# Narrower scatter targets, spread sums and separate last input tiles in a fused attention, expert and feed-forward kernel

## The chip, the cores and the metric

The kernel runs on one core of one Trainium2 chip. The metric is the device time of one execution in microseconds (us); the kernel before has a median of 876.0 us in three runs. Engines are called as the profile calls them: PE (TensorE matmul), DVE (VectorE), ACT (ScalarE), POOL (GpSimd), SP (SyncE, which here only issues DMAs).

## The reference

Three layers follow one another on 2304 tokens (4 sequences of 576) with 512 features: block-causal attention, a layer of 8 experts of which each token takes one, and a dense feed-forward layer with a softplus.

```python
def reference(q, k, v, w_gate, w1, w2, w_in, w_out):
    x = attention(q, k, v)            # 4 x 8 heads, 576 positions, blocks of 64, softmax
    x = x.transpose(0, 2, 1, 3).reshape(2304, 512)
    e = argmax(x @ w_gate, axis=1)    # one expert of 8 for each token
    x = gate_w * (relu(x @ w1[e]) @ w2[e])
    h = x @ w_in                      # 512 -> 2048
    g = maximum(h, 0) + log1p(exp(-abs(h)))
    return g @ w_out                  # 2048 -> 512
```

## The kernel before

All products are made of three matmuls on split operands (high and low part in fp32r): high x high, low x high, high x low. The order of all work is written out by hand in one string of step names, `SCHEDULE`; each name calls one step, and the instructions of a step go to their engines in that order. Pools of named tiles give the buffers; an instruction that writes a tile waits for the last readers of the tile that had the buffer before.

The change lies in the feed-forward layer (`ffn`), the last 410 us. Tokens stand in 18 tiles of 128, which are worked on in five groups: groups 0 to 3 have four tiles each, group 4 has two. In steps called after the group `g`:

- `Pg.f.k` are the matmuls of the first layer for the 16 column blocks `f`, `ag.f.0` to `.2` three activations on ACT (L1242, L1244, L1246), `ag.f.3` the maximum and sum on DVE (L1248), `ag.f.4` the store of the block to a scratch tensor `gd` in DRAM by SP (L1250). The five `ft` tiles go round.
- The second layer is a 2 x 2 scheme with seven products instead of eight. For each of the 8 chunks `c`, `Ng.c.0` loads two blocks of `gd` back into a tile `gq` (two DMAs of SP, L1346), `.1` to `.3` form the sums on DVE (L1352 for the first; L1355 and L1356; L1358), `.4` casts to high parts `ah` on ACT (L1365, L1367) and `.5` forms the low parts `al` on DVE (L1369, L1372). `Qg.c.m` are the seven products on PE. `W` steps load converted weights for it (SP, L1332).
- `og.u.i` combine the products on ACT and DVE (L1405 copies a PSUM bank to a tile `fy`; L1413, L1416, L1418, L1422 write `fos`), `Og.u.j` write the result. For groups 0 to 3 that is a scatter by an indirect DMA of POOL, four in a row for each group (L1430), whose row indices stand in `OI`. For group 4 it is four plain stores of 128 x 256 to rows 2048 to 2303 of `out`, three by SP and one by ACT (L1427).

A tile `gq` takes one of three buffers in turn. Chunks 3 to 5 of group 4 use the second halves of the tiles of chunks 0 to 2, so that chunk 6 gets the buffer that chunks 0 and 3 had, and chunk 7 that of chunks 1 and 4. A scatter names the whole of `out` as its target, so an instruction that writes any part of `out` waits until the scatters before it have landed.

Of the kernel before, what the change touches and what calls it, by code (L numbers as in the profile page):

```python
# [7 lines left out]
F32 = mybir.dt.float32  # L8
# [12 lines left out]
NT, DM, E, F1, F2 = 2304, 512, 8, 1024, 2048  # L21
# [192 lines left out]
a4.6.4 W4.4 W4.5 P4.8.3 a4.7.2 P4.9.0 a4.7.3 a4.8.0 P4.9.1 a4.8.1 a4.7.4 W4.6 W4.7 P4.9.2 a4.8.2 P4.9.3 P4.10.0 a4.8.3  # L214
a4.9.0 P4.10.1 a4.8.4 W4.8 W4.9 a4.9.1 P4.10.2 a4.9.2 P4.10.3 P4.11.0 a4.9.3 a4.10.0 P4.11.1 a4.9.4 W4.10 W4.11 a4.10.1
P4.11.2 a4.10.2 P4.11.3 P4.12.0 a4.10.3 a4.11.0 P4.12.1 a4.10.4 W4.12 W4.13 a4.11.1 P4.12.2 a4.11.2 P4.12.3 P4.13.0
a4.11.3 a4.12.0 P4.13.1 a4.11.4 a4.12.1 P4.13.2 a4.12.2 P4.13.3 P4.14.0 a4.12.3 a4.13.0 P4.14.1 a4.12.4 W5.0 W5.1
a4.13.1 P4.14.2 a4.13.2 P4.14.3 P4.15.0 a4.13.3 N0.2.1 N0.2.2 N0.2.3 a4.14.0 P4.15.1 a4.13.4 W5.2 W5.3 a4.14.1 P4.15.2
a4.14.2 P4.15.3 Q0.0.0 a4.14.3 a4.15.0 a4.14.4 W5.4 W5.5 a4.15.1 Q0.0.1 a4.15.2 a4.15.3 Q0.0.2 a4.15.4 W5.6 e2 N0.1.4
N0.1.5 N0.2.4 N0.4.0 W5.7 W5.8 W5.9 N0.3.1 N0.3.2 N0.3.3 N0.2.5 N0.5.0 W5.10 W5.11 W5.12 W5.13 W6.0 Q0.0.3 Q0.0.4  # L220
Q0.0.5 Q0.0.6 Q0.1.0 N0.3.4 Q0.1.1 N0.4.1 N0.4.2 N0.4.3 Q0.1.2 N0.3.5 N0.6.0 W6.1 W6.2 W6.3 Q0.1.3 Q0.1.4 Q0.1.5 Q0.1.6
# [23 lines left out]
N3.6.5 N4.1.0 N4.3.0 N4.4.0 Q3.4.3 Q3.4.4 Q3.4.5 Q3.4.6 Q3.5.0 N3.7.4 Q3.5.1 N4.0.1 N4.0.2 N4.0.3 Q3.5.2 N3.7.5 N4.2.0  # L245
N4.5.0 Q3.5.3 Q3.5.4 Q3.5.5 Q3.5.6 Q3.6.0 N4.0.4 Q3.6.1 N4.1.1 N4.1.2 N4.1.3 Q3.6.2 N4.0.5 Q3.6.3 Q3.6.4 Q3.6.5 Q3.6.6
Q3.7.0 N4.1.4 N4.2.1 N4.2.2 N4.2.3 N4.1.5 Q3.7.1 o3.0.0 o3.1.0 Q3.7.2 Q3.7.3 o3.0.1 o3.0.2 o3.1.1 o3.1.2 Q3.7.4 Q3.7.5
o3.0.3 o3.1.3 Q3.7.6 o3.0.4 O3.0.0 O3.0.1 o3.1.4 O3.1.0 O3.1.1 Q4.0.0 N4.2.4 Q4.0.1 N4.3.1 N4.3.2 N4.3.3 Q4.0.2 N4.2.5
Q4.0.3 Q4.0.4 Q4.0.5 Q4.0.6 Q4.1.0 N4.3.4 Q4.1.1 N4.4.1 N4.4.2 N4.4.3 Q4.1.2 N4.3.5 N4.6.0 Q4.1.3 Q4.1.4 Q4.1.5 Q4.1.6
Q4.2.0 N4.4.4 Q4.2.1 N4.5.1 N4.5.2 N4.5.3 Q4.2.2 N4.4.5 N4.7.0 Q4.2.3 Q4.2.4 Q4.2.5 Q4.2.6 Q4.3.0 N4.5.4 Q4.3.1 N4.6.1  # L250
N4.6.2 N4.6.3 Q4.3.2 N4.5.5 Q4.3.3 Q4.3.4 Q4.3.5 Q4.3.6 Q4.4.0 N4.6.4 Q4.4.1 N4.7.1 N4.7.2 N4.7.3 Q4.4.2 N4.6.5 Q4.4.3
Q4.4.4 Q4.4.5 Q4.4.6 Q4.5.0 N4.7.4 Q4.5.1 N4.7.5 Q4.5.2 Q4.5.3 Q4.6.0 Q4.6.1 Q4.6.2 Q4.6.3 Q4.7.0 Q4.7.1 o4.0.0 Q4.7.2
Q4.7.3 o4.0.1 O4.0.1 O4.0.2 o4.0.2 Q4.5.4 Q4.5.5 Q4.6.4 Q4.6.5 Q4.7.4 Q4.7.5 o4.0.3 Q4.5.6 Q4.6.6 Q4.7.6 o4.0.4 O4.0.0
# [932 lines left out]
def ffn(tc, P, yd, gd, wd, w_in, w_out, HB, OI, out, ident):  # L1186
# [7 lines left out]
    st = {}  # L1194
# [76 lines left out]
    QW = 256  # L1271
# [63 lines left out]
    def chunk(g, c, i):  # L1335
        w = 128 * groups[g][1]
        q = w // 2
        n = 8 * g + c
        if i == 0:
            p, tag = (P["pa"], f"gq{n % 3}") if n % 3 < 2 else (P["hlb"], "U2")  # L1340
            if g == 4 and 3 <= c < 6:
                t = st["g", g, c] = st["g", g, c - 3][:, :, w:2 * w]
            else:
                t = st["g", g, c] = p.tile([128, 2, 512], F32, tag=tag, name=f"gq{n % 3}", bufs=1)
            for j in range(2):
                nc.sync.dma_start(t[:, j, 0:w], gd[16 * g + c + 8 * j, :, 0:w])  # L1346
            return
        t = st["g", g, c]
        quarter = lambda h, a: t[:, h, q * a:q * a + q]
        if i == 1:  # L1350
            s = st["gs", g, c] = sums(n)
            TT(s[:, 0:w], t[:, 0, 0:w], t[:, 1, 0:w], op=ALU.add)  # L1352
        elif i == 2:
            s = st["gs", g, c]
            TT(s[:, w:w + q], quarter(0, 1), quarter(0, 0), op=ALU.subtract)  # L1355
            TT(s[:, w + q:2 * w], quarter(1, 0), quarter(1, 1), op=ALU.subtract)  # L1356
        elif i == 3:
            TT(st["gs", g, c][:, 2 * w:2 * w + q], quarter(0, 0), quarter(1, 1), op=ALU.add)  # L1358
        else:
            if i == 4:  # L1360
                st["gp", g, c] = part_tiles(n % 3)
            s = st["gs", g, c][:, 0:5 * q]
            h, l = st["gp", g, c]
            if i == 4:
                nc.scalar.copy(h[:, 0:5 * q], s)  # L1365
                for j in range(2):
                    nc.scalar.copy(h[:, (5 + j) * q:(6 + j) * q], quarter(j, j))  # L1367
            else:
                TT(l[:, 0:5 * q], s, h[:, 0:5 * q].bitcast(F32), op=ALU.subtract)  # L1369
                for j in range(2):  # L1370
                    e = slice((5 + j) * q, (6 + j) * q)
                    TT(l[:, e], quarter(j, j), h[:, e].bitcast(F32), op=ALU.subtract)  # L1372
# [51 lines left out]
    def done(g, u, j):  # L1424
        if g == 4:
            i, o = groups[g][0] + j // 2, QW * (j % 2)
            (nc.scalar if j == 3 else nc.sync).dma_start(out[128 * i:128 * i + 128, o:o + QW], st["out", g, u][:, j])  # L1427
            return
        i = groups[g][0] + groups[g][1] // 2 * j + u
        nc.gpsimd.indirect_dma_start(  # L1430
            out=out, out_offset=bass.IndirectOffsetOnAxis(ap=OI[:, i:i + 1], axis=0),
            in_=st["out", g, u][:, 2 * j:2 * j + 2].rearrange("p a b -> p (a b)"), in_offset=None,
            bounds_check=NT - 1, oob_is_err=False,
        )

    calls = {}
# [185 lines left out]
```

## Time and profile before

| | us |
|---|---|
| median of three runs | 876.0 (875.87 to 878.16) |
| the profiled execution: its time | 877.16 |
| the profiled execution: its span | 875.5 |
| PE busy | 861.2 (98%) |
| DVE busy | 667.5 (76%) |
| ACT busy | 559.6 (64%) |
| POOL busy | 124.2 (14%) |

The span runs from the first to the last instruction of the core; 1.7 us of the profiled execution's time lie outside of it. PE's clock was granted in full from beginning to end (each of the 40 slices of the profile shows a 9). A row of the timeline has the start and the duration in us, the engine, the line, the operation, what it writes and reads, and in brackets the idle time of that engine before it with what ended it. An engine name with a q (SPq, POOLq) is its sequencer: waits, DMA issues and the closing instructions of the program stand there.

### The profile page before, as it was taken

The numbers are of one execution on the slowest core, as the hardware profiler recorded it, in microseconds if no ns is written. First come the engines' busy times: TensorE is split into PE (matmuls) and PEld (weight loads), VectorE is DVE, ScalarE is ACT, GpSimd is POOL, SyncE is SP. The second block draws the span as 40 slices with busy tenths as digits, with TensorE's granted clock in tenths as the row PEclk, the third lists the DMA queues.
The fourth block names the chain that finished last, engine by engine and source line by source line (L and its number), as shares of the span: only waits on it lengthen the run. The fifth ranks groups of instructions, "written<-read, shape, count | busy, mean of one in ns | idle before, by whom it ended". The sixth has DMA issues, their size and how long they took to land.

```text
span 875.5 us, 17767 instructions
## 1 busy us (share of the span) xinstructions
PE 861.2 (98%) x5974; PEld 754.4 (86%) x5974; DVE 667.5 (76%) x1627; ACT 559.6 (64%) x1236; POOL 124.2 (14%) x149
## 2 busy tenths in 40 slices
PE   8999999999999999999999999999999999999997
PEld 5778777877899899998998888878889999999997
DVE  5787789977999888665963768667775589897966
ACT  6677777786665767655854878878888643343432
POOL 3010000011032142211311000000000003150302
PEclk9999999999999999999999999999999999999999
DMA  6976196124427398765461566457755884533422
GB/s 135 175 155 139 43 177 187 50 87 143 163 76 228 111 310 277 267 222 193 120 229 39 179 225 215 147 181 251 263 213 210 266 290 128 162 118 127 142 74 97
DMA packets 141941, 149.15 MB, mean 170 GB/s; under 512 B 73487, under 2 KB 99087, under 8 KB 141840
## 3 DMA queue, kind: packets, MB, share of 16 engines
q1 hardware_dynamic: 135696, 132.80, 50.1%
q0 software_dynamic: 4800, 14.70, 4.8%
q8 instruction: 49, 0.80, 0.4%
q10 hardware_dynamic: 1344, 0.43, 0.2%
q14 instruction: 52, 0.43, 0.2%
HBM read 120.09 MB, written 41.43 MB: 184 GB/s over the span
## 4 chain that ended last, share of the span: by engine, by line
PE 65%; DMA 1%; ACT 0%; SPq 0%; issue 0%; DVE 0%; DVEq 0%; ACTq 0%
PE yps L1090 4%; PE yps L1092 4%; PE yps L1091 3%; PE fh L1233 3%; PE fh L1234 3%; PE fh L1232 3%; PE hps L1056 3%; PE hps L1057 3%; PE hps L1055 3%; PE fz L1399 3%; PE fz L1397 3%; PE fz L1398 3%; PE fX L1233 2%; PE fX L1234 2%; PE fX L1232 2%; PE fY L1233 2%
## 5 line engine op out<-in xcount | busy, mean ns | idle before, releaser
L1365 ACT CAST ah<-sum 128x1280 fp32r<-128x1280 f32 (+1 forms) x40 | 46.3, 1158 | 103.1 <-issue 39.4
L410 ACT ACTIVATE P<-s,negm 128x192 f32<-128x192 f32 (+4 forms) x160 | 83.6, 526 | 39.1 <-DVE negm L402 33.8
L1055 PE MATMUL hps<-xh,H1h 128*128 128x256 f32 x320 | 90.7, 283 | 0.0
L1057 PE MATMUL hps<-xh,H1l 128*128 128x256 f32 x320 | 90.5, 283 | 0.0
L1056 PE MATMUL hps<-xl,H1h 128*128 128x256 f32 x320 | 90.5, 283 | 0.0
L402 DVE CUSTOM_DVE_ANT_0 s<-s,mask 128x576 f32<-128x576 f32 (+3 forms) x128 | 70.1, 569 | 26.4 <-PE s L392 23.5
L1011 DVE TENSOR_TENSOR H2l<-R,H2h 128x512 fp32r<-128x512 f32 x96 | 63.7, 686 | 24.9 <-ACT H2h L1007 21.3
L1007 ACT CAST H2h<-R 128x512 fp32r<-128x512 f32 x96 | 57.5, 623 | 28.8 <-PE yps L1091 14.1
L1090 PE MATMUL yps<-H2h,hh 128*128 128x512 f32 x176 | 71.5, 406 | 0.4 <-PEq L1562 0.4
L1430 POOL DMA_INDIRECT out_dram<-fos,OI x16 | 41.0, 2561 | 204.8 <-DVE fos L1422 166.5
L1091 PE MATMUL yps<-H2h,hl 128*128 128x512 f32 x176 | 68.8, 391 | 0.0
L1092 PE MATMUL yps<-H2l,hh 128*128 128x512 f32 x176 | 68.7, 391 | 0.0
L1011 DVE TENSOR_TENSOR H1l<-R,H1h 128x512 fp32r<-128x512 f32 x96 | 62.4, 684 | 8.3 <-ACT H1h L1007 6.3
L1369 DVE TENSOR_TENSOR al<-sum,ah 128x1280 fp32r<-128x1280 f32 (+1 forms) x40 | 54.1, 1352 | 16.9 <-ACT ah L1365 16.9
L1007 ACT CAST H1h<-R 128x512 fp32r<-128x512 f32 x96 | 55.5, 622 | 16.4 <-PE hps L1056 10.3
L420 PE MATMUL pt<-ident,P 128*128 128x128 f32 x400 | 61.1, 281 | 2.1 <-DVE PT L426 0.8
L1056 PEld LDWEIGHTS hps<-xl,H1h 128*128 128x128 f32 x320 | 61.4, 192 | 0.3
L1055 PEld LDWEIGHTS hps<-xh,H1h 128*128 128x128 f32 x320 | 61.3, 192 | 0.3
L1057 PEld LDWEIGHTS hps<-xh,H1l 128*128 128x128 f32 x320 | 61.4, 192 | 0.0
L392 PEld LDWEIGHTS s<-kZ,qZ 64*128 64x128 f32 x576 | 47.3, 185 | 14.0 <-ACT P L410 5.5
L392 PE MATMUL s<-kZ,qZ 64*128 64x288 f32 (+4 forms) x576 | 56.1, 312 | 1.0 <-DVE kZ L367 0.6
L420 PEld LDWEIGHTS pt<-ident,P 128*128 128x128 f32 x400 | 44.3, 141 | 11.1 <-DVE PT L426 4.4
(366 smaller groups left out, 2606.6 us busy)
## 6 DMA issues: line engine op xcount, KB each, us to landing
R<-in_moe_w_dram SPq DMA_DIRECT2D x96, 512.0 KB
gd<-ft SPq DMA_DIRECT2D x64, 256.0 KB
gq<-gd SPq DMA_DIRECT2D x64, 256.0 KB
dbw<-in_moe_w_out_dram SPq DMA_DIRECT2D x32, 256.0 KB
dbl<-in_moe_w_in_dram SPq DMA_DIRECT2D x22, 256.0 KB
yg<-yd SPq DMA_DIRECT2D x4, 1026.0 KB
xd<-xs SPq DMA_DIRECT2D x16, 256.0 KB
wd<-ah SPq DMA_DIRECT2D x4, 896.0 KB
```

Source lines behind the costliest of these rows:

```text
L392: mm(o, lhsT=a, rhs=b, start=first, stop=last)
L402: nc.vector.tensor_tensor_reduce(x, x, MASK[:, S - NK[c]:S], scale=1.0, scalar=3.0e38, op0=ALU.add, op1=ALU.min, accum_out=m)
L410: nc.scalar.activation(t, x, AF.Exp, bias=NM.pop((p, j, c))[0:n], scale=-1.0, accum_out=rs[p % 4][0:n, c, j:j + 1])
L420: nc.tensor.transpose(ps[:, 128 * i:128 * i + 128], PB[p % NPB][c][:, a:a + 128], ident)
L1007: nc.scalar.copy(HW[l, i][0], raw(l, i))
L1011: TT(l_, raw(l, i), h.bitcast(F32), op=ALU.subtract)
L1055: mm(a, lhsT=wh, rhs=xh, start=(k == 0), stop=False)
L1056: mm(a, lhsT=wh, rhs=xl, start=False, stop=False)
L1057: mm(a, lhsT=wl, rhs=xh, start=False, stop=(k == 3))
L1090: mm(o, lhsT=h[:, c], rhs=wh, start=(f == 0), stop=False)
L1091: mm(o, lhsT=l[:, c], rhs=wh, start=False, stop=False)
L1092: mm(o, lhsT=h[:, c], rhs=wl, start=False, stop=(f == 7))
```

## The change

It has three parts. The scatters name only rows 0 to 2047 of `out` as target, and their bound on an index is 2047. In group 0, the four sums of chunk 2 (`N0.2.1` to `N0.2.3`), which stood in a row behind `a4.13.3`, stand one step each behind `a4.11.3`, `a4.12.3` and `a4.13.3`. And the inputs of chunks 6 and 7 of group 4 get tiles of 128 x 2 x 256 under the tag of the two `fy` buffers, with their loads `N4.6.0` and `N4.7.0` at the start of the products of group 4, behind the scatters of group 3.

```diff
-a4.11.3 a4.12.0 P4.13.1 a4.11.4 a4.12.1 P4.13.2 a4.12.2 P4.13.3 P4.14.0 a4.12.3 a4.13.0 P4.14.1 a4.12.4 W5.0 W5.1
-a4.13.1 P4.14.2 a4.13.2 P4.14.3 P4.15.0 a4.13.3 N0.2.1 N0.2.2 N0.2.3 a4.14.0 P4.15.1 a4.13.4 W5.2 W5.3 a4.14.1 P4.15.2
+a4.11.3 N0.2.1 a4.12.0 P4.13.1 a4.11.4 a4.12.1 P4.13.2 a4.12.2 P4.13.3 P4.14.0 a4.12.3 N0.2.2 a4.13.0 P4.14.1 a4.12.4
+W5.0 W5.1 a4.13.1 P4.14.2 a4.13.2 P4.14.3 P4.15.0 a4.13.3 N0.2.3 a4.14.0 P4.15.1 a4.13.4 W5.2 W5.3 a4.14.1 P4.15.2
...
-o3.0.3 o3.1.3 Q3.7.6 o3.0.4 O3.0.0 O3.0.1 o3.1.4 O3.1.0 O3.1.1 Q4.0.0 N4.2.4 Q4.0.1 N4.3.1 N4.3.2 N4.3.3 Q4.0.2 N4.2.5
+o3.0.3 o3.1.3 Q3.7.6 o3.0.4 O3.0.0 O3.0.1 o3.1.4 O3.1.0 O3.1.1 N4.6.0 N4.7.0 Q4.0.0 N4.2.4 Q4.0.1 N4.3.1 N4.3.2 N4.3.3
...
             if g == 4 and 3 <= c < 6:
                 t = st["g", g, c] = st["g", g, c - 3][:, :, w:2 * w]
+            elif g == 4 and c > 5:
+                t = st["g", g, c] = P["p2"].tile([128, 2, QW], F32, tag="fy", name="gq3", bufs=2)
...
         nc.gpsimd.indirect_dma_start(
-            out=out, out_offset=bass.IndirectOffsetOnAxis(ap=OI[:, i:i + 1], axis=0),
+            out=out[0:NT - 256], out_offset=bass.IndirectOffsetOnAxis(ap=OI[:, i:i + 1], axis=0),
             in_=st["out", g, u][:, 2 * j:2 * j + 2].rearrange("p a b -> p (a b)"), in_offset=None,
-            bounds_check=NT - 1, oob_is_err=False,
+            bounds_check=NT - 257, oob_is_err=False,
```

On DVE, at the end of the first layer of group 4 (L1248 is the sum `a4.f.3`; the four lines that read `gq` are the sums of chunk 2 of group 0), the rows stand before the change as

```order
L1248 SCALAR_TENSOR_TENSOR ft<-fh,ft 128x256
L1248 SCALAR_TENSOR_TENSOR ft<-fY_12744,ft 128x256
L1248 SCALAR_TENSOR_TENSOR ft<-fX_12765,ft 128x256
L1352 TENSOR_TENSOR sum_12811<-gq_12657 128x512
L1355 TENSOR_TENSOR sum_12811<-gq_12657 128x256
L1356 TENSOR_TENSOR sum_12811<-gq_12657 128x256
L1358 TENSOR_TENSOR sum_12811<-gq_12657 128x256
```

and with it, two lines further down in the source, as

```order
L1248 SCALAR_TENSOR_TENSOR ft<-fh,ft 128x256
L1354 TENSOR_TENSOR sum_12770<-gq_12657 128x512
L1248 SCALAR_TENSOR_TENSOR ft<-fY_12744,ft 128x256
L1357 TENSOR_TENSOR sum_12770<-gq_12657 128x256
L1358 TENSOR_TENSOR sum_12770<-gq_12657 128x256
L1248 SCALAR_TENSOR_TENSOR ft<-fX_12765,ft 128x256
L1360 TENSOR_TENSOR sum_12770<-gq_12657 128x256
```

The first sum has moved in front of the last but one `ft` row shown, the next two in front of the last, and one stays behind it; nothing else on DVE has moved.

On SP, the last DMAs of the program (two loads each for chunks 6 and 7 of group 4, then the three stores; DMASW are the semaphores of POOL's DMAs, DMAHW those of SP's and ACT's) stand before the change as

```order
L1346 DMA gq_14956<-gd 128x256 [waits DMAHW6_49,DMAHW5_49,DVE_49]
L1346 DMA gq_14956<-gd 128x256
L1346 DMA gq_14993<-gd 128x256 [waits DMAHW7_49,DMAHW0_49,DVE_49]
L1346 DMA gq_14993<-gd 128x256
L1427 DMA out_dram<-fos 128x256 [waits DMASW4_49,DMASW5_49,DMASW3_49,DMASW6_49,DMASW2_49,DMASW7_49,DMASW1_49,DMAHW1_49,DMASW0_49,DVE_49]
L1427 DMA out_dram<-fos 128x256 [waits DMAHW2_49]
L1427 DMA out_dram<-fos 128x256 [waits DMAHW3_49,DVE_49]
```

and with it as

```order
L1348 DMA gq_14896<-gd 128x256 [waits DMAHW5_49,DVE_49,Activation_49]
L1348 DMA gq_14896<-gd 128x256 [waits DMAHW6_49]
L1348 DMA gq_14899<-gd 128x256 [waits DMAHW7_49,DVE_49,Activation_49]
L1348 DMA gq_14899<-gd 128x256 [waits DMAHW0_49]
L1429 DMA out_dram<-fos 128x256 [waits DMAHW1_49,DVE_49]
L1429 DMA out_dram<-fos 128x256 [waits DMAHW2_49]
L1429 DMA out_dram<-fos 128x256 [waits DMAHW3_49,DVE_49]
```

The order on SP is the same; the loads wait for the `fy` tiles of group 3 in place of the older `gq` tiles, and the stores no longer wait for any scatter. ACT's one store loses the same waits. The scatters of POOL keep theirs: each still waits for the one before it.

## Rows read from the trace of the kernel before

**Rows 1.** Windows: each engine's busy us, instruction count, PE clock, DMA share, GB/s.
```profile
690.00:692.00 2.00, 1.08 (x9) 1.08 (x10) 0.84 (x2) 2.00 (x4) 0.00 (x0) 1.00 0.88 262
692.00:870.00 178.00, 178.00 (x1490) 178.00 (x1489) 151.59 (x317) 69.88 (x124) 40.98 (x16) 1.00 0.46 149
```

**Rows 2.** Timeline around PE's one gap, 685 to 691 us: PE, ACT, SP, DVE.
```profile
690.92 0.39 PE L1397 MATMUL fX<-Wh,ah 128*128 128x256 f32 x1 [1.00 <-DVE ft L1248]
...
689.12 0.38 ACT L1242 ACTIVATE ft<-fX 128x256 f32<-128x256 f32 x1 [0.72 <-DMA gd<-ft]
...
686.02 0.38 SPq L1250 DMA_DIRECT2D gd<-ft  x1
...
685.95 0.42 DVE L1248 SCALAR_TENSOR_TENSOR ft<-fY,ft 128x256 f32<-128x256 f32 x1 [0.74 <-ACT ft L1246]
687.12 0.43 DVE L1248 SCALAR_TENSOR_TENSOR ft<-fX,ft 128x256 f32<-128x256 f32 x1 [0.75 <-ACT ft L1246]
687.46 0.68 DVE L1352 TENSOR_TENSOR sum<-gq 128x512 f32<-128x512 f32 x1
```

**Rows 3.** The last stores: SP's wait (total, times, longest), issues, DVE's last work.
```profile
SPq L1427 <- DMA out_dram<-fos,OI: 11.1, 1, 11.1
...
870.32 0.75 DVE L1422 TENSOR_TENSOR fos<-fw,fz 128x256 f32<-128x256 f32 x2 [0.38 <-PE fz L1399]
871.37 1.31 SPq L1427 DMA_DIRECT2D out_dram<-fos  x3
871.41 0.38 ACTq L1427 DMA_DIRECT2D out_dram<-fos  x1
```

**Rows 4.** The program's closing instructions: ns shortest/median/longest, first and last start.
```profile
L1617 POOLq EVENT_SEMAPHORE  x4: 17/17/17, 874.7 to 875.4; - x4
L1617 POOLq DRAIN  x3: 40/113/5882, 868.5 to 875.2; - x3
L1617 SPq DRAIN  x3: 7/7/13, 874.6 to 874.9; - x3
```

**Rows 5.** Timeline of POOL: the second scatter of group 0, the four of group 3.
```profile
736.82 9.11 POOL L1430 DMA_INDIRECT out_dram<-fos,OI  x1 [2.53 <-DMA out_dram<-fos,OI]
...
852.68 0.98 POOL L1430 DMA_INDIRECT out_dram<-fos,OI  x1 [21.15 <-DVE fos L1422]
856.21 3.80 POOL L1430 DMA_INDIRECT out_dram<-fos,OI  x1 [2.54 <-DVE sum L1358]
863.44 1.31 POOL L1430 DMA_INDIRECT out_dram<-fos,OI  x1 [3.43 <-DVE sum L1358]
868.39 0.98 POOL L1430 DMA_INDIRECT out_dram<-fos,OI  x1 [3.63 <-DVE fos L1413]
```

**Rows 6.** Timeline of DVE beside the second scatters of groups 0 and 3.
```profile
745.40 0.69 DVE L1352 TENSOR_TENSOR sum<-gq 128x512 f32<-128x512 f32 x1 [0.33 <-DMA gq<-gd]
...
858.67 0.48 DVE L1372 TENSOR_TENSOR al<-gq,ah 128x128 fp32r<-128x128 f32 x2
859.87 0.43 DVE L1352 TENSOR_TENSOR sum<-gq 128x256 f32<-128x256 f32 x1 [0.72 <-DMA gq<-gd]
...
864.22 0.82 DVE L1369 TENSOR_TENSOR al<-sum,ah 128x640 fp32r<-128x640 f32 x1
864.96 0.48 DVE L1372 TENSOR_TENSOR al<-gq,ah 128x128 fp32r<-128x128 f32 x2
```

**Rows 7.** Windows inside the second scatters of groups 0 and 3, as in rows 1.
```profile
737.40:745.00 7.60, 7.60 (x65) 7.60 (x65) 7.60 (x15) 2.71 (x7) 7.60 (x1) 1.00 0.44 140
...
857.00:859.10 2.10, 2.10 (x20) 2.10 (x19) 2.10 (x8) 1.15 (x4) 2.10 (x1) 1.00 0.40 111
```

**Rows 8.** Timeline: PE's first product of chunk 5, ACT's cast for chunk 7.
```profile
862.62 0.28 PE L1397 MATMUL fY<-W,ah 128*128 128x256 f32 x1
...
863.27 0.73 ACT L1365 CAST ah<-sum 128x640 fp32r<-128x640 f32 x1 [1.13 <-DVE sum L1358]
```

**Rows 9.** The last scatter alone, from its start to its landing.
```profile
DMA to landing us min/median/max: 2.7/2.7/2.7
```

More of the change, by code (lines that the diff above doesn't have):

```diff
@@ L247 @@
 Q3.7.0 N4.1.4 N4.2.1 N4.2.2 N4.2.3 N4.1.5 Q3.7.1 o3.0.0 o3.1.0 Q3.7.2 Q3.7.3 o3.0.1 o3.0.2 o3.1.1 o3.1.2 Q3.7.4 Q3.7.5
-o3.0.3 o3.1.3 Q3.7.6 o3.0.4 O3.0.0 O3.0.1 o3.1.4 O3.1.0 O3.1.1 Q4.0.0 N4.2.4 Q4.0.1 N4.3.1 N4.3.2 N4.3.3 Q4.0.2 N4.2.5
-Q4.0.3 Q4.0.4 Q4.0.5 Q4.0.6 Q4.1.0 N4.3.4 Q4.1.1 N4.4.1 N4.4.2 N4.4.3 Q4.1.2 N4.3.5 N4.6.0 Q4.1.3 Q4.1.4 Q4.1.5 Q4.1.6
-Q4.2.0 N4.4.4 Q4.2.1 N4.5.1 N4.5.2 N4.5.3 Q4.2.2 N4.4.5 N4.7.0 Q4.2.3 Q4.2.4 Q4.2.5 Q4.2.6 Q4.3.0 N4.5.4 Q4.3.1 N4.6.1
+o3.0.3 o3.1.3 Q3.7.6 o3.0.4 O3.0.0 O3.0.1 o3.1.4 O3.1.0 O3.1.1 N4.6.0 N4.7.0 Q4.0.0 N4.2.4 Q4.0.1 N4.3.1 N4.3.2 N4.3.3
+Q4.0.2 N4.2.5 Q4.0.3 Q4.0.4 Q4.0.5 Q4.0.6 Q4.1.0 N4.3.4 Q4.1.1 N4.4.1 N4.4.2 N4.4.3 Q4.1.2 N4.3.5 Q4.1.3 Q4.1.4 Q4.1.5
+Q4.1.6 Q4.2.0 N4.4.4 Q4.2.1 N4.5.1 N4.5.2 N4.5.3 Q4.2.2 N4.4.5 Q4.2.3 Q4.2.4 Q4.2.5 Q4.2.6 Q4.3.0 N4.5.4 Q4.3.1 N4.6.1
 N4.6.2 N4.6.3 Q4.3.2 N4.5.5 Q4.3.3 Q4.3.4 Q4.3.5 Q4.3.6 Q4.4.0 N4.6.4 Q4.4.1 N4.7.1 N4.7.2 N4.7.3 Q4.4.2 N4.6.5 Q4.4.3
```

## The prediction, made before the changed kernel ran

> **What bounds the kernel now.** I read the windows first. From 692 to 870 us PE is busy without a break; in the 2 us before it loses 0.92 [rows 1]. A change of order on other engines can therefore give back only that gap and what lies behind PE's last matmul. Next I read the timeline around the gap, then the closing instructions, and then the timelines of POOL and DVE side by side, since the change touches the scatters and what DVE waits for beside them.
>
> The gap: PE's product waits 1.00 us for the last `ft` sum on DVE, which follows three activations on ACT, the first of which waited 0.72 us for the store of an older `ft` tile; SP had issued that store at 686.02 [rows 2]. The end: DVE ends at 870.32 + 0.75 = 871.07. SP, which could have stored two of the four blocks before, waited 11.1 us for the scatters, issued its three stores from 871.37 to 872.68 [rows 3] and reached its closing instruction at 874.6, 1.9 us behind the last issue. POOL's closing DRAIN began at 868.5, just behind the last scatter, took 5.88 us and so ended at 874.35; POOL's next instruction stands at 874.7, with SP then the last to come [rows 4]. So POOL was only 0.3 us ahead of SP.
>
> **Part 1, the stores.** Without the waits two stores go out at about 868, and the last one is ACT's: DVE's end 871.07, some 0.1 for the semaphore, 0.38 of issue, 1.9 of landing, 873.5 in place of 874.6. On SP's side that is a gain of 1.1 us. But the program ends when POOL is through too: if its DRAIN still ends at 874.35, only 0.3 of the 1.1 are left. What ends next is thus POOL's DRAIN. The trace does not show what it waits for. I take it as bound to the last scatter, because it begins there and SP's DRAIN beside it takes 7 to 13 ns [rows 4]; the other bound is that it ends with whatever transfer ends last.
>
> **Part 2, the spread sums.** The four sums that stood in a row go into the gaps of 0.74 and 0.75 us in front of two `ft` sums [rows 2]: 0.68 for the first, and for the next two, each half as wide, no more than that together. They fit, and no `ft` sum comes later. The sum behind them (`a4.14.3`) comes up to 0.7 earlier, but the last one does not: it hangs on ACT, which waits for SP's store, and neither moves. So PE's gap stays, and the part is worth 0. If the fit fails, an `ft` sum comes 0.1 late, which ACT's own 0.72 of idle time covers. The load of this `gq` stands on SP ahead of the store at 686.02, behind which SP lags, so DVE gains no wait.
>
> **Part 3, the tiles of chunks 6 and 7.** Their loads, now so late that DVE waits 0.72 us for one up to 859.87 [rows 6], go out once the combining of group 3 has read `fy`, which is before the first scatter starts at 852.68 [rows 5]. SP has nothing else between them and the stores. DVE then loses that wait; PE has no gap there [rows 1], so this alone gives 0. But that idle time has a second user, POOL.
>
> The second scatter of group 3 started at 856.21 and took 3.80 us where a free one takes 0.98 [rows 5]. It ended at 860.01, that is 0.86 us behind 859.87 - 0.72 = 859.15, the moment DVE went idle [rows 6]. In group 0 the second scatter took 9.11 us and ended at 745.93; DVE had gone idle at 745.40 - 0.33 = 745.07 [rows 5, 6], 0.86 before. Groups 1 and 2 show the same twice more. In between DVE ran 15 and 8 instructions end to end, and PE and ACT were no busier than elsewhere [rows 7]. So in this kernel a second scatter got through when DVE paused, four times of four, and the change removes the pause that let it through in group 3.
>
> The Trainium skill speaks of this place. Its page "SBUF — State Buffer", section "Who interferes with whom", says that a VectorE instruction with two SBUF inputs contends with a GpSimd instruction that reads SBUF, and that the one issued second blocks until the first finishes. By this rule the scatter would start at the end of the one instruction that DVE was in, within a microsecond, and part 3 would cost nothing, which is rival D. The trace agrees that the two contend, but here the scatter stood back for 8 to 15 DVE instructions in the windows shown, not for one.
>
> Where does DVE pause next? Its stream moves up by 0.72, so that the low parts of chunk 7 come at 863.5 in place of 864.22 [rows 6]. They need ACT's cast of that chunk, 0.73 long, now at 863.27. Its sums would let it start at 862.55, but its tile is free only when PE is through with chunk 4, whose successor begins at 862.62 [rows 8], plus some 0.2 until the last product is out and the semaphore seen. So the cast runs from about 862.8 to 863.5, and DVE pauses for 0.1 us or so at about 863.4. I let the scatter through there: 4.25 us later than 859.15, ending at 864.3. The next scatter started 3.43 behind it with loads of `gq` beside it, and 2.55 in the pair before, without them; I take 3.0, hence 867.3. From there to the fourth it was 4.95 with a hold of 0.33 in it, against 3.53 for the free link from the first to the second [rows 5]; I take 3.5, since DVE's work at 867 follows PE with pauses: 870.8 in place of 868.39, 2.4 us later. Bounds: 2.55 + 3.5 gives 870.35, 3.43 + 4.95 gives 872.7. POOL's DRAIN then ends at 870.85 + 5.88 = 876.75, and the span 0.8 behind it (874.7 to 875.5 [rows 4]): 877.55. That is 2.1 us more than 875.5.
>
> **The sum.** The profiled execution took 877.16, 1.16 above the median; I put differences on the median. Part 2: 0. Part 1: -0.3 with POOL's DRAIN in its place, included in the 877.55. Part 3: +2.4. Together 876.0 + 2.1 = 878.1, +0.24%. About 0.3%, 2.6 us, is what can be told from no change here.
>
> **Case A (chance 0.33), the forecast: 878.1.** The scatters slip to 863.4, and the DRAIN carries it to the end. For it: four scatters of four, and the DRAIN's place. Against it: a DRAIN of 5.88 us appears once only.
>
> **Case B (0.19), slower: 879.4.** The pause at 863.4 is too short. In group 0 it took one of 0.33 us to let a scatter through [rows 6], mine is an estimate of 0.1. Then the scatter gets through when DVE's last low parts end, 864.96 + 0.48 - 0.72 = 864.7, 1.3 later than in A: 879.4, with slow links up to 881. It decides whether ACT's cast comes at least 0.3 us late for DVE. Against it: the third scatter of group 3 took 1.31, though DVE ran end to end beside it, so a scatter sometimes gets in without a pause.
>
> **Case C (0.20): 875.2.** The scatters slip, but the DRAIN does not follow them. The last one lands at 870.8 + 2.7 [rows 9] = 873.5, with the last store; SP closes 0.9 earlier than now: 875.1, and up to 876.3 with B's slip. For it: the DRAIN ended within 0.3 us of the last store's landing.
>
> **Case D (0.22): 875.7.** The second scatter gets in at about 859 without the pause; the chain stays, and the end moves up by the 0.3 us that POOL was ahead (up to 1.1 if the DRAIN follows the stores: 874.9). For it: the skill's rule and the third scatter's 1.31. Against it: four of four.
>
> **Case E (0.06):** the gap at 690 closes by chance of the transfers, up to -0.9 on top of C or D, or widens by as much. It is 0.92 us long [rows 1], so neither sign is reached by it alone.
>
> **How the numbers follow.** A is the likeliest: 878.1. Of A a tenth or two lies above 878.6, of B nearly all; C and D lie within 2.6 us of 876.0. Slower by over 0.3%: 0.24; within 0.3%: 0.71; faster: 0.05 (D with the full 1.1 and the closed gap would just reach it). The range takes in C and D, A with its bounds and the lower half of B: 874.9 to 879.6.
>
> **What would show it right or wrong.** In the profile after: SP's first store at about 868 without a wait (part 1; else the narrowed target did nothing). DVE's pause at 859 gone, and the second scatter of group 3 ending near 864.3 (A), 865.5 (B) or 860 (D). The last scatter's start near 870.8 and a DRAIN of some 5.9 us behind it (A, B), or one that ends with the stores (C). PE's gap at 690 still about 1 us (part 2). The forecast is wrong if the fourth scatter starts by 868.5, or if the DRAIN shrinks as the scatters slip.

## The result, and the profile after

The changed kernel takes 881.51 us (median of five runs, 880.56 to 881.86), the kernel before 876.73 (median of five runs, 875.87 to 878.16). The ratio is 1.0051, with a 95% interval from 1.0039 to 1.0063: 4.8 us slower, 3.4 to 5.5 by the interval. The forecast was 878.1 (+0.24%) with a range up to 879.6; measured is +0.51%. The sign was among those given (slower: 0.24, though "within 0.3%" was the likeliest), the size was not.

The profiled execution of the changed kernel took 880.94 us and its span is 879.2. Engine totals first, from the page (busy us, share of the span, instructions):

```profile
PE 862.0 (98%) x5974; PEld 754.9 (86%) x5974; DVE 666.8 (76%) x1627; ACT 559.6 (64%) x1236; POOL 129.2 (15%) x149
```

PE does what it did; POOL has 5.0 us more. Most of that, 4.16 us, is the second scatter of group 3 in POOL's timeline, from 845 us on, which answers to [rows 5] (start and duration in us, engine, line, operation, in brackets the idle time before it and what ended it):

```profile
853.69 0.98 POOL L1432 DMA_INDIRECT out_dram<-fos,OI  x1 [21.20 <-DVE fos L1424]
857.23 7.96 POOL L1432 DMA_INDIRECT out_dram<-fos,OI  x1 [2.56 <-DVE sum L1360]
868.60 0.98 POOL L1432 DMA_INDIRECT out_dram<-fos,OI  x1 [3.41 <-DMA out_dram<-fos,OI]
872.44 0.98 POOL L1432 DMA_INDIRECT out_dram<-fos,OI  x1 [2.86 <-DVE fos L1424]
```

The second scatter takes 7.96 us in place of 3.80 and ends at 865.19. Beside it DVE, which answers to [rows 6], and the cast on ACT that it waits for, to [rows 8]:

```profile
863.84 0.48 DVE L1374 TENSOR_TENSOR al<-gq,ah 128x128 fp32r<-128x128 f32 x2
864.63 0.82 DVE L1371 TENSOR_TENSOR al<-sum,ah 128x640 fp32r<-128x640 f32 x1 [0.30 <-ACT ah L1367]
...
863.87 0.73 ACT L1367 CAST ah<-sum 128x640 fp32r<-128x640 f32 x1 [1.36 <-PE fz L1401]
```

DVE's pause at chunk 6 is gone. Its next one is the 0.30 us before the low parts of chunk 7, from 864.33 on, and the scatter ended 0.86 us behind that moment: the same distance as in [rows 5, 6]. The end of the program answers to [rows 3, 4]. SP's three stores in the timeline:

```profile
868.90 3.21 SPq L1429 DMA_DIRECT2D out_dram<-fos  x3
```

The closing instructions (ns shortest/median/longest, first and last start):

```profile
L1619 POOLq EVENT_SEMAPHORE  x4: 17/17/17, 878.4 to 879.1; - x4
L1619 POOLq DRAIN  x3: 40/113/5883, 872.5 to 879.0; - x3
L1619 SPq DRAIN  x3: 7/7/13, 876.1 to 878.7; - x3
```

And what SP waited for behind its stores, the landing of the last scatter (us in total, times, longest):

```profile
SPq L1619 <- DMA out_dram<-fos,OI: 3.3, 1, 3.3
```

SP's first store goes out at 868.90 without a wait for a scatter. POOL's DRAIN starts at 872.5, just behind the start of the last scatter (872.44), takes 5.883 us (before: 5.882) and ends at 878.4. SP reaches its own closing DRAIN at 876.1, 2.3 us earlier. So SP waits for POOL here; before, POOL was the one that was through first.

PE's last product is the other half of the comparison. Its start in the kernel before:

```profile
870.00 0.28 PE L1399 MATMUL fz<-Wl,ah 128*128 128x256 f32 x1
```

And in the changed kernel:

```profile
871.01 0.28 PE L1401 MATMUL fz<-Wl,ah 128*128 128x256 f32 x1
```

From there to the end of the span, called the **tail** from here on, it is 875.47 - 870.00 = 5.47 us in the profile of before and 879.24 - 871.01 = 8.23 us in that of after: 2.76 of the 3.77 us between the two spans. The other 1.0 us is older than the whole feed-forward layer. The window from 14 to 19 us of the kernel before (each engine's busy us and instruction count, PE's granted clock, DMA share, GB/s):

```profile
14.00:19.00 5.00, 4.51 (x39) 3.49 (x38) 4.58 (x19) 4.39 (x16) 0.00 (x0) 1.00 0.51 106
```

The same window of the changed kernel:

```profile
14.00:19.00 5.00, 4.63 (x29) 3.34 (x30) 3.16 (x15) 3.82 (x14) 0.00 (x0) 0.66 0.49 102
```

And of the kernel before in a second profile, which is told of below:

```profile
14.00:19.00 5.00, 4.56 (x27) 3.07 (x27) 3.30 (x14) 3.82 (x14) 0.00 (x0) 0.66 0.49 102
```

In the last two the granted clock is 0.66 of full speed in the mean: it stood at the lower of its two levels (1.2 GHz) for some 3.4 of the 5 us, though PE had been busy for 10.5 to 10.7 of the first 14 us in all three. Of each kernel there is one profile with this drop and one without. So it is no work of the change, and it shifts everything behind it by about 1 us. The tail does not depend on it, which is why the experiments below are compared by tail as well as by time.

### The profile page after: what moved, and what is told of

Same layout as the page of the kernel before. It is cut to its first block, busy times and chain, and to the rows that moved or that the text cites. A ratio compares the mean times of both kernels' runs of the same rounds, so it can differ in the third digit from the quotient of the medians.

```text
span 879.2 us, 17761 instructions
## 1 busy us (share of the span) xinstructions
PE 862.0 (98%) x5974; PEld 754.9 (86%) x5974; DVE 666.8 (76%) x1627; ACT 559.6 (64%) x1236; POOL 129.2 (15%) x149
## 4 chain that ended last, share of the span: by engine, by line
PE 59%; DMA 3%; ACT 2%; DVE 1%; issue 1%; SPq 0%; POOL 0%; DVEq 0%; ACTq 0%
PE yps L1090 4%; PE yps L1092 3%; PE yps L1091 3%; PE hps L1056 3%; PE hps L1057 3%; PE hps L1055 3%; PE fz L1401 3%; PE fz L1399 3%; PE fz L1400 3%; PE fh L1233 2%; PE fh L1234 2%; PE fh L1232 2%; PE fX L1399 2%; PE fX L1400 2%; PE fX L1401 2%; PE fY L1399 2%
## 5 line engine op out<-in xcount | busy, mean ns | idle before, releaser
L1432 POOL DMA_INDIRECT out_dram<-fos,OI x16 | 45.5, 2845 | 203.7 <-DVE fos L1424 169.2
```

## Experiments

**The theory** before them: part 3 alone costs. It takes away the pause of DVE in which the second scatter got through, the scatters slip, and POOL's DRAIN, 5.88 us long and bound to the last scatter, carries the slip to the end. **Rivals**: part 1 or part 2 costs something by itself; the end is set by whatever transfer is last and not by the last scatter; part of the 4.8 us has nothing to do with the end, since the profiles explain only 2.76 there.

### One part at a time, and the changed kernel again

Part 1 alone, on the kernel before:

```diff
-            out=out, out_offset=bass.IndirectOffsetOnAxis(ap=OI[:, i:i + 1], axis=0),
+            out=out[0:NT - 256], out_offset=bass.IndirectOffsetOnAxis(ap=OI[:, i:i + 1], axis=0),
...
-            bounds_check=NT - 1, oob_is_err=False,
+            bounds_check=NT - 257, oob_is_err=False,
```

> The kernel before with part 1 alone (the scatters name rows 0 to 2047). Theory (the end is POOL's closing DRAIN, 5.88 us behind the start of the last scatter): the scatters of group 3 stay where they were, the last one starts near 868.4, the DRAIN ends near 874.35, and the span is 0.3 us shorter than 875.5; on the median -0.3 us, which cannot be told from nothing. Rival (SP's stores alone set the end): -1.1 us, span 874.4. Second rival (part 1 itself is what costs): slower than before by over 2 us.

Part 2 alone (in SCHEDULE, the step names that moved):

```diff
-... a4.11.3 a4.12.0 ... a4.12.3 a4.13.0 ... a4.13.3 N0.2.1 N0.2.2 N0.2.3 ...
+... a4.11.3 N0.2.1 a4.12.0 ... a4.12.3 N0.2.2 a4.13.0 ... a4.13.3 N0.2.3 ...
```

> The kernel before with part 2 alone (three sums of chunk 2 of group 0 spread). Theory: 0.0 us, PE's gap near 690 us stays at 0.9 to 1.1 us and the end as before. Rival (the measured +4.8 us has a part that the end does not show, up to 2 us, and it comes from here): +1 to +2 us, with a wider gap near 690 or a difference further ahead.

Part 3 alone:

```diff
-... O3.1.1 Q4.0.0 ... N4.3.5 N4.6.0 Q4.1.3 ... N4.4.5 N4.7.0 Q4.2.3 ...
+... O3.1.1 N4.6.0 N4.7.0 Q4.0.0 ... N4.3.5 Q4.1.3 ... N4.4.5 Q4.2.3 ...
...
+            elif g == 4 and c > 5:
+                t = st["g", g, c] = P["p2"].tile([128, 2, QW], F32, tag="fy", name="gq3", bufs=2)
```

> The kernel before with part 3 alone (small tiles and early loads for chunks 6 and 7 of group 4). Theory: the second scatter of group 3 waits for DVE's pause near 863.4 and takes about 8 us, the last one starts near 871.4, SP's stores wait for its landing at 874.1 and POOL's DRAIN ends near 877.4: span +2.7 us. Rival (only the parts together cost): within 0.5 us of before.

The changed kernel, unchanged, beside them:

> The changed kernel once more, beside the three single parts. In its profile PE's clock stood at half from about 15 to 18 us, which no instruction of the change touches, and its product ran 0.9 us late from there on. Theory: that dip comes and goes from one execution to the next, in either kernel; without it the difference is the 2.7 us of the end, so +3 to +4 us on the median. Rival (the dip belongs to the changed kernel): +4.8 us again, the dip in its profile and none in those of the three single parts.

| | median us (runs) | ratio to before | 95% interval | tail, us |
|---|---|---|---|---|
| before, same chip | 876.38 (23) | | | |
| part 1 alone | 876.94 (12) | 1.0007 | 0.9995 to 1.0018 | 4.03 |
| part 2 alone | 877.51 (11) | 1.0010 | 0.9996 to 1.0024 | 6.45 |
| part 3 alone | 880.01 (5) | 1.0040 | 1.0027 to 1.0053 | 8.28 |
| all three again | 880.81 (5) | 1.0052 | 1.0039 to 1.0065 | 8.12 |

Part 3 alone carries the loss, parts 1 and 2 can't be told from nothing. PE's gap near 690 us is 0.70 us with part 2 alone and 1.09 in the changed kernel, against 1.00 in [rows 2]; it wanders and part 2 does not close it. With part 3 alone the second scatter took 7.96 us again, and SP, which still waits for the scatters there, ends last with POOL close to it. With all three the clock of the second profile stayed full at 14 to 19 us and the loss was the same: the dip is not its cause.

The closing rows of part 1 alone, in the form of [rows 4]:

```profile
L1617 POOLq DRAIN  x3: 40/113/5886, 867.9 to 874.9; - x3
L1617 SPq DRAIN  x3: 7/7/13, 874.3 to 874.6; - x3
```

Those of part 3 alone:

```profile
L1619 POOLq DRAIN  x3: 40/113/5886, 871.3 to 878.0; - x3
L1619 SPq DRAIN  x3: 7/7/13, 877.4 to 877.7; - x3
```

The DRAIN is 5.886 us both times, 3.3 us apart in time, each some 0.1 us behind the start of its last scatter (867.87 and 871.22). With part 1 alone it is over at 873.8, and SP, whose closing DRAIN starts at 874.3, ends last: the theory of that run, that POOL's DRAIN ends it, did not hold there.

What these runs did not fit: the tail of before is 5.47, with part 1 alone it is 4.03, with part 2 alone, which touches nothing there, 6.45. The expected -0.3 for part 1 came out as -1.44 in the tail, and the median did not move. Something at the end of the kernel before varies by itself.

### The kernel before, a second profile

> The kernel before, a second profile. The differences so far are 4.4 to 4.8 us for the changed kernel, while the ends of the profiles explain 2.7: from the start of PE's last product to the end of the span it is 5.47 us in the profile of before and 8.1 to 8.3 with part 3. Theory: the first profile of before caught an execution (877.16 us, the median is 876.4) whose last scatter was late, at 868.39 with 3.64 us between the third scatter's end and its start where the run with part 1 alone shows 2.57; a usual execution ends about 4.2 us behind PE's last start, so that the end explains 4 us. Rival: 5.5 us again, and the rest of the difference lies ahead of the end.

PE's last product starts at 871.04 (this is the profile with the lower clock at 14 to 19 us), and the tail is 875.07 - 871.04 = 4.03 us. The four scatters of group 3 in it, to be read against [rows 5]:

```profile
853.31 0.98 POOL L1430 DMA_INDIRECT out_dram<-fos,OI  x1 [17.18 <-DVE fos L1422]
856.84 3.79 POOL L1430 DMA_INDIRECT out_dram<-fos,OI  x1 [2.55 <-DVE sum L1358]
863.97 0.99 POOL L1430 DMA_INDIRECT out_dram<-fos,OI  x1 [3.34 <-DMA out_dram<-fos,OI]
867.47 0.98 POOL L1430 DMA_INDIRECT out_dram<-fos,OI  x1 [2.52 <-DMA out_dram<-fos,OI]
```

The third scatter is not held (0.99 where [rows 5] have 1.31) and the fourth follows 2.52 us behind it where [rows 5] have 3.63. So the last scatter starts 3.57 us ahead of PE's last product, against 1.61 in the profile that the prediction rested on, and with part 2 alone 0.64 (link 4.61). In the kernel before these scatters then no longer hold up the end: SP's first two stores still wait for them but go out ahead of PE's end, at 870.47 and 870.86, the other two behind DVE's work, and the tail is the same 4.03 as with part 1 alone. The first profile of before had caught a late chain. How rare that is, the times say: in the three later comparisons the kernel before has 24 executions whose mean granted clock is 1.000, as in its first profile, and 22 of them took less than that profile's 877.16 us; their median is 876.1. Against a tail of 4.03, the 8.12 to 8.28 of part 3 are 4.1 to 4.2 us, which lies inside the measured 3.4 to 5.5. The rival (a loss ahead of the end) isn't needed, and the profiles without the drop of the clock speak against it: PE's last product starts at 870.00 in the kernel before, at 870.03 with part 3 alone and at 869.57 with all three parts.

What made the third scatter land 1.1 to 2.1 us later in those two executions was not tried, but the traces show what lay beside it. DMA queues in the first profile of before, from 865.10 to 867.20 us, while the third scatter's packets ran (packets, MB, share of 16 engines):

```profile
q0 software_dynamic: 80, 0.26, 33.6%
q8 instruction: 1, 0.02, 3.4%
```

And in the second profile, from 865.50 to 866.40:

```profile
q0 software_dynamic: 80, 0.26, 77.0%
```

In the first a packet of 16 KB on the instruction queue started at 865.14 and took 1.15 us, and the scatter's 80 packets took 1.84 us in place of 0.84; with part 2 alone one started at 865.53, and they took 2.81. In the second profile of before, and with part 1 alone, that packet started as the scatter's last ones ended. In these four profiles it starts 3.8 to 4.9 us ahead of PE's last product. That it is what delayed the scatter is read from this order alone; no run moved it.

### Giving the pause back

The changed kernel with another order on DVE: the low parts of chunks 3, 4 and 5 move ahead, so that those of chunks 4 and 5 stand close behind the sums whose cast they need.

```diff
-... N4.3.4 Q4.1.1 N4.4.1 N4.4.2 N4.4.3 Q4.1.2 N4.3.5 Q4.1.3 ...
+... N4.3.4 Q4.1.1 N4.3.5 N4.4.1 N4.4.2 N4.4.3 Q4.1.2 Q4.1.3 ...
-... Q4.2.0 N4.4.4 Q4.2.1 N4.5.1 N4.5.2 N4.5.3 Q4.2.2 N4.4.5 ... N4.6.1 N4.6.2 N4.6.3 Q4.3.2 N4.5.5 ...
+... Q4.2.0 N4.4.4 N4.4.5 Q4.2.1 N4.5.1 N4.5.2 N4.5.3 Q4.2.2 ... N4.6.1 N4.5.5 N4.6.2 N4.6.3 Q4.3.2 ...
```

> The changed kernel with another order on DVE at chunks 4 and 5 of group 4: the low parts stand directly behind the sums whose cast on ACT they need, so that DVE stands idle for 0.5 to 0.9 us at about 858.1 and 861.4 (on the clock of the changed kernel's profile). Theory (a scatter that waits gets in when DVE pauses): the second scatter ends near 859.0 and takes 1.7 us in place of 8, the last one starts at 865 to 868, and the end is that of the stores; PE may lose up to 0.4 us at chunk 6, whose low parts come late. 3.5 to 4 us less than the changed kernel. Rival (the scatters' lateness is not what costs): as the changed kernel, or slower by the 0.4 us.

876.29 us (12 runs) against 877.02 of before on that chip (23 runs): ratio 0.9990, from 0.9980 to 0.9999. That is 4.5 to 5.2 us below the two medians of the changed kernel, which were taken on other chips (5.4 us by the ratios). POOL's scatters, and DVE's first pause (the third scatter starts in the second one, 0.54 us long):

```profile
851.31 0.98 POOL L1432 DMA_INDIRECT out_dram<-fos,OI  x1 [17.59 <-DVE fos L1424]
854.85 1.71 POOL L1432 DMA_INDIRECT out_dram<-fos,OI  x1 [2.56 <-DVE al L1374]
859.09 0.99 POOL L1432 DMA_INDIRECT out_dram<-fos,OI  x1 [2.53 <-DVE sum L1354]
862.59 1.41 POOL L1432 DMA_INDIRECT out_dram<-fos,OI  x1 [2.52 <-DVE sum L1360]
...
855.42 0.28 DVE L1360 TENSOR_TENSOR sum<-gq 128x128 f32<-128x128 f32 x1
856.57 0.83 DVE L1371 TENSOR_TENSOR al<-sum,ah 128x640 fp32r<-128x640 f32 x1 [0.87 <-ACT ah L1367]
```

DVE goes idle at 855.70, and the second scatter, started at 854.85, ends at 856.56: 0.86 behind, as always. 1.71 us were expected at 1.7. The last scatter starts 6.5 us ahead of PE's last product, and the tail is 4.02. Nothing else of the change was touched: tiles, early loads and narrow targets are all still there. So the loss is the lost pause, and the rival (the lateness of the scatters costs nothing) falls.

### Without the pause: an instruction that reads no SBUF

The changed kernel with a memset of 128 x 1 behind the sums and behind the low parts of chunks 3 to 7 of group 4:

```diff
+    def rest():
+        if "scr" not in st:
+            st["scr"] = P["pa"].tile([128, 1], F32, tag="scr", name="scr", bufs=1)
+        nc.vector.memset(st["scr"], 0.0)
...
+        if g == 4 and c >= 3 and i in (3, 5):
+            rest()
```

> The changed kernel with a memset of 128 x 1 on DVE behind the sums and behind the low parts of chunks 3 to 7 of group 4, ten in all, of some 0.06 us each. Theory 1 (an instruction of DVE that reads no SBUF lets the waiting scatter in): the second scatter of group 3 gets through near 858.1 and takes about 1.7 us in place of 8, the last one starts near 866 to 867, and the end is that of SP's stores, some 4.2 us behind PE's last start: 4 us less than the changed kernel, about as before. Theory 2 (DVE must stand idle): the second scatter takes 7.6 to 8.5 us as in the changed kernel, and the time is its, +-0.5 us.

873.98 us (12 runs; before 877.02), ratio 0.9971, from 0.9958 to 0.9984: faster than both kernels, by more than either theory said. POOL and DVE:

```profile
850.56 0.98 POOL L1439 DMA_INDIRECT out_dram<-fos,OI  x1 [20.48 <-DVE fos L1431]
854.09 1.33 POOL L1439 DMA_INDIRECT out_dram<-fos,OI  x1 [2.54 <-DVE scr L1338]
857.94 0.98 POOL L1439 DMA_INDIRECT out_dram<-fos,OI  x1 [2.52 <-DMA out_dram<-fos,OI]
861.45 1.55 POOL L1439 DMA_INDIRECT out_dram<-fos,OI  x1 [2.53 <-DVE scr L1338]
...
853.74 0.82 DVE L1376 TENSOR_TENSOR al<-sum,ah 128x640 fp32r<-128x640 f32 x1
853.76 0.06 DVE L1338 MEMSET scr<- 128x1 f32 x1
854.48 0.48 DVE L1379 TENSOR_TENSOR al<-gq,ah 128x128 fp32r<-128x128 f32 x2
```

The second scatter needs 1.33 us. It did not even wait for the next memset, at 854.92: it ended at 855.42, 0.86 us behind the end of the one instruction of DVE in which it had started (853.74 + 0.82 = 854.56). Tail 4.04. Why a memset ahead of that instruction lets the scatter in at its end, while in the changed kernel the same instruction and 22 more behind it kept it out, these runs don't tell.

The time has a second term that nobody had expected. PE's last product starts at 867.69, 1.4 us earlier than in any other run so far, and the tail can't do that. The products of the second layer run faster, as a window of nothing but products, from 700 to 850 us, shows by their count (the first pair is PE's). The changed kernel:

```profile
700.00:850.00 150.00, 150.00 (x1256) 150.00 (x1256) 127.60 (x255) 58.69 (x98) 34.62 (x12) 1.00 0.47 155
```

This one:

```profile
700.00:850.00 150.00, 150.00 (x1270) 150.00 (x1269) 129.68 (x259) 59.84 (x101) 36.50 (x12) 1.00 0.47 154
```

That is 150 / 1256 = 119.4 ns for one against 118.1 (those that reach over an edge of the window are counted too). No memset stands in that window. But the scratch tile is 32 bytes of SBUF in the pool of the sums, and it moves the sums, `ah` and `al` by 32 bytes against the weights. Two runs take the two apart.

The memsets in a pool that moves nothing:

```diff
-            st["scr"] = P["pa"].tile([128, 1], F32, tag="scr", name="scr", bufs=1)
+            st["scr"] = P["scr"].tile([128, 1], F32, tag="scr", name="scr", bufs=1)
...
-            P.update(p2=pool("fin2", "p2", side="right"), wrest=pool("fin2", "wrest", side="right"))
+            P.update(p2=pool("fin2", "p2", side="right"), wrest=pool("fin2", "wrest", side="right"), scr=pool("fin2", "scr", side="right"))
```

> The run with ten memsets was 7 us quicker than the changed kernel, where 4 were expected: its end is 4.04 us behind PE's last start (changed kernel 8.1 to 8.2), as expected, but its products of the second layer also run at 118.3 ns each in place of 119.6, 1.9 us over 1485 of them. The scratch tile of the memsets lies in the pool of the sums and moves the tiles of ah, al and the sums down by 32 bytes a partition against the weights of chunks 0 to 5. Here the same memsets write a tile in a pool of its own that moves no other tile. Theory: products at 119.6 ns, last scatter near 6.2 us ahead of PE's last start, end 4.0 us behind it: 4.1 us less than the changed kernel, 876 to 877 us. Rival (the memsets themselves quicken PE): 118.3 ns again and 874 us.

The 32 bytes without the memsets beside the scatters:

```diff
-        if g == 4 and c >= 3 and i in (3, 5):
+        if g == 4 and c == 7 and i == 5:
             rest()
```

> The changed kernel with the scratch tile alone (it moves ah, al and the sums by 32 bytes; one memset behind the last low parts, where no scatter waits). Theory: products of the second layer at 118.3 ns, PE ends 1.9 us earlier, the second scatter of group 3 takes 8 us and the end lies 8.1 us behind PE's last start as in the changed kernel: 878.5 to 879 us. Rival (the place of the tiles is nothing): 119.6 ns and 880.8 us.

On the same chip (before 876.32, 23 runs):

| | median us (runs) | ratio to before | 95% interval | tail, us | products from 700 to 850 us |
|---|---|---|---|---|---|
| memsets, nothing moved | 875.68 (12) | 0.9990 | 0.9981 to 1.0000 | 4.03 | 1256 |
| 32 bytes, no memset | 878.22 (11) | 1.0014 | 1.0004 to 1.0024 | 8.24 | 1267 |

Both came out as the theory said, to 0.3 us. The memsets alone mend the tail (second scatter 1.32 us, last one 6.4 us ahead of PE's last product) and leave PE as it was; the 32 bytes alone quicken PE and leave the tail at 8.24 with a second scatter of 7.97 us.

### The other end: how long is the DRAIN when the last scatter is far from the end

The changed kernel without the second to fourth scatter of group 3:

```diff
         i = groups[g][0] + groups[g][1] // 2 * j + u
+        if g == 3 and u + j:
+            return
```

> The changed kernel without the second to fourth scatter of group 3 (384 rows of the output are left unwritten). Theory (the DRAIN runs 5.88 us from the last scatter on): it starts at about 853.7, is over by 859.7, and the span ends 4.0 to 4.3 us behind PE's last start, with SP's stores. Rival (the DRAIN waits for whatever is last on any queue, or POOL's closing takes some 5.9 us whenever it comes): 8.1 us behind PE's last start, as now.

```profile
L1621 POOLq DRAIN  x3: 40/113/5938, 851.7 to 873.0; - x3
L1621 SPq DRAIN  x3: 7/7/7, 872.3 to 872.6; - x3
```

The DRAIN starts at 851.7, beside the one scatter (851.89), still takes 5.94 us and is over at 857.6; the span ends at 873.2, with SP, 4.01 us behind PE's last product. So the DRAIN follows POOL's last scatter and no other transfer, and its price is about 5.9 us whether the last stores are near or far. POOL's other DRAINs in the same profile take 0.18 us, at the program's start, and 0.11 and 0.04, behind the long one, so not every DRAIN costs that; a program without any scatter was not run. In eleven of the thirteen profiles the DRAIN ended 4.97 to 4.98 us behind the end of the last scatter, also where that scatter was held: there the DRAIN itself was longer, off the path (6.45 us with the first memsets, beside a scatter of 1.55). With the two pauses it took 7.51 us and ended 6.18 behind; why, no run tells.

The same profile shows that a pause is not the only way in. The second scatter of group 0 in it, and DVE beside its end:

```profile
735.14 5.42 POOL L1434 DMA_INDIRECT out_dram<-fos,OI  x1 [2.53 <-DMA out_dram<-fos,OI]
...
738.95 0.75 DVE L1374 TENSOR_TENSOR al<-gq,ah 128x256 fp32r<-128x256 f32 x2
739.62 0.68 DVE L1354 TENSOR_TENSOR sum<-gq 128x512 f32<-128x512 f32 x1
```

In every other profile this scatter took 9.1 us, up to DVE's next pause. Here it ended 0.86 us behind the end of a pair of low parts, with DVE's next instruction already running. Group 1 shows the same, 8.58 us in place of 10.2.

### A version that beats both

The memsets with the 32 bytes, and 32 bytes more between the first expert weights and the tokens, and between `ah`, `al` and the weights of chunks 6 and 7:

```diff
-            P.update(hw1=pool("moe", "hw1", side="right"), gat=...
+            P.update(hw1=pool("moe", "hw1", side="right"), pad=pool("moe", "pad", side="right"), gat=...
+            nc.vector.memset(P["pad"].tile([128, 1], F32, name="pad", bufs=1), 0.0)
...
-            P.update(p2=pool("fin2", "p2", side="right"), wrest=pool("fin2", "wrest", side="right"))
+            P.update(p2=pool("fin2", "p2", side="right"), wpad=pool("fin2", "wpad", side="right"), wrest=pool("fin2", "wrest", side="right"))
+            nc.vector.memset(P["wpad"].tile([128, 1], F32, name="wpad", bufs=1), 0.0)
```

> The ten memsets with the shift of 32 bytes, and 32 bytes more in two other places: between the first expert weights H1h, H1l and the tokens xh, xl (960 products at 120.0 ns, both now at the same place modulo 64 bytes), and between the tiles of ah, al and the weights of chunks 6 and 7. Theory (products run at exactly 120.0 ns where their two operands lie alike modulo 64 bytes, and at some 117.8 where they don't): the expert products fall to 117 to 118.5 ns, 1.5 to 2.9 us, and chunks 6 and 7 give another 0.5 us: 871 to 872.5 us. Rival (it is particular to the second layer): 874 us as with the memsets alone.

871.11 us (5 runs) against 876.32: ratio 0.9930, from 0.9917 to 0.9944. The expert products in the kernel before, as groups (busy us, mean ns of one, idle time before; PE is the product, PEld its weight load):

```profile
L1055 PE MATMUL hps<-xh,H1h 128*128 128x256 f32 x320 | 90.7, 283 | 0.0
L1055 PEld LDWEIGHTS hps<-xh,H1h 128*128 128x128 f32 x320 | 61.3, 192 | 0.3
```

Here:

```profile
L1055 PE MATMUL hps<-xh,H1h 128*128 128x256 f32 x320 | 90.2, 282 | 0.6 <-DVE hl L1075 0.6
L1055 PEld LDWEIGHTS hps<-xh,H1h 128*128 128x128 f32 x320 | 60.3, 188 | 1.1 <-DVE hl L1075 0.8
```

And the window of products, here:

```profile
700.00:850.00 150.00, 150.00 (x1279) 150.00 (x1279) 130.88 (x265) 59.47 (x101) 42.94 (x13) 1.00 0.47 156
```

A weight load takes 188 ns in place of 192, and the second layer is down to 150 / 1279 = 117.3 ns for a product. The time between the starts of two expert products, with pauses left out, fell from 119.9 to 118.3 ns in the mean. The shift of 32 bytes is borne out in three places; the modulus in the expectation is not, since the weights of chunks 4 and 5 lie like `ah` modulo 64 bytes and their products ran at 118.75 ns before any shift. (The distances come from the addresses that the built programs give the tiles; the traces don't have them.) Nor is the distance the whole: chunks 0 to 3 have the same one with the 32 bytes alone, with the first memsets and here, and their products ran at 117.8, 117.6 and 116.7 ns. What else has moved them is open.

## Why the prediction was wrong, point by point

- **Part 1**: right as to the stores. SP's first store goes at 868.90, on PE's time 867.9, with 868 foreseen. That POOL's DRAIN ends next holds in the changed kernel, but not with part 1 alone, where SP ended last. Its worth of 0.3 us was read from an execution whose last scatter was late; in a usual one it is 0, since a kernel with part 1 and a kernel without it both have a tail of 4.03.
- **Part 2**: right. 0, and the gap at 690 stays.
- **Part 3, where DVE pauses next**: right to 0.1 us. The scatter got in at 864.33; PE ran 1.01 us late in that profile, so 863.3 on the time of before, with 863.4 foreseen, and the pause of 0.30 us was enough. Case B feared that 0.1 would not be; with the 32 bytes alone the same pause was 0.12 us, and the scatter got in. Counted from PE's last product, the second scatter ends at -5.8, with -5.7 foreseen.
- **Part 3, the two links behind it**: mis-sized by 0.6 us. From the second scatter's end to the third's start 3.1 to 3.5 us, where I took 3.0; from the third's start to the fourth's 3.50 to 4.00, where I took 3.5, the link of an undisturbed pair, though the row for this very pair had 4.95. The last scatter starts 1.2 to 1.4 us behind PE's last product, not 0.8, and the tail is 8.12 to 8.28, not the 877.55 - 870.00 = 7.55 of the sum. The traces show something beside both links, though no run removed it: in each profile with part 3 and no remedy the 16 KB on the instruction queue lie ahead of the second scatter's packets, which take 1.35 to 1.73 us in place of 0.84; and with part 1 SP's first stores run beside the third scatter's packets. With part 3 alone, where the stores wait, the last link is the 3.50 foreseen, with all three parts it is 3.84 and 4.00.
- **The DRAIN**: right. 5.88 to 5.94 us in ten profiles, in which the last scatter started anywhere between 851.9 and 872.4. Cases C (875.2 in its heading, 875.1 by its sum) and D fall. D's rule is that of the Trainium skill, page "SBUF — State Buffer", section "Who interferes with whom": of a VectorE and a GpSimd instruction that contend, the second blocks until the first finishes. The trace agrees for the third scatter of [rows 5], which got in at the end of one instruction, and for the run with memsets. It disagrees for the second scatter of the changed kernel, which stood back for 23 instruction ends, in each of the four profiles that have part 3 without a remedy.
- **The step that failed is "I put differences on the median".** The end of the profiled execution, tail 5.47, was itself 1.44 us longer than a usual end of this kernel, by a scatter that landed late. The changed end was worked out absolutely, from links taken to hold in any execution, and then compared with that long end. That the profiled execution lay 1.16 us above the median was seen and treated as a constant that cancels; it was part of the very stretch that the change rewrites. Against the usual tail the effect is 4.1 to 4.2 us; of the 2.1 us between that and the forecast, 1.4 are this base and 0.6 the two links.
- **What is left**: 881.51 - 876.73 = 4.8 and, in the second comparison, 4.4 us, against 4.1 to 4.2. The difference lies within the intervals. PE's clock at 14 to 19 us adds up to 1 us to single executions of either kernel.
- **The range** ended at 879.6 because it was built on case B with the same short links and the same base, so it shared the error. It did not even take in case A with its bounds, as it says: with the fourth scatter at the upper bound, 872.7, the sum gives 878.1 + 1.9 = 880.0. On the time of before the fourth scatter started at 871.4, inside those bounds. That B's 879.4 lies nearest of the cases is luck, since what B describes did not happen. On the usual tail case A would have read 876.0 + 7.55 - 4.03 = 879.5.

## What to carry to other kernels

An idle moment of DVE can be what another engine lives on: before a wait of DVE is taken away beside a software DMA of POOL, look for who gets in at that moment, and leave a pause, or an instruction that reads no SBUF, where it is needed. A program's last scatter from POOL should start some 6 us before the last plain store lands, as POOL's closing DRAIN took 5.9 us from there in ten profiles and 6.4 to 7.5 in the other three. And an end that is compared with one profiled execution wants a second profile of the same kernel first: here two of them differed by 1.4 us in just the stretch that mattered.

## What the runs showed of the hardware that was not expected

- A scatter that doesn't get in at the end of the DVE instruction in which it starts stayed out through 7 to 22 more in most cases (25 at most), back to back with two SBUF inputs each. Of the 51 second scatters of a group in the thirteen profiles 46 ended 0.85 to 0.87 us behind a moment at which DVE went idle; the pause there was 0.30 us in the changed kernel, and pauses of 0.03 to 0.12 us were enough elsewhere. Three, with the memsets, got in at the end of the instruction in which they started, and two, told of above, at the end of a later one without a pause. In the first profiles of before and after, of the twenty-four first, third and fourth scatters none stayed out for more than two ends; in five other runs one third scatter was held for 5.2 to 5.5 us. What tells them apart is open.
- Products of 128 x 128 by 128 x 256 in fp32r started every 119.9 ns in the mean (pauses left out) where the two operands' tiles lie a multiple of 512 bytes apart in SBUF (weights of chunks 0 to 3, 6 and 7 and `ah`; expert weights and `xh`), every 118.75 with the weights of chunks 4 and 5 (128 bytes off such a multiple), and every 116.7 to 118.7 with 32 bytes more between. 32 bytes of padding in three places were worth 4 to 5 us of 876 here (875.68 to 871.11 between the two runs with memsets). Which distances are good was not mapped.
